# Linear attention and a gated feed-forward network on one core: the gates of the last four chunks as two pairs with seven block products instead of eight

## The chip, the cores and the metric

One NeuronCore of a Trainium2 chip runs the kernel. Its engines are TensorE (PE, matrix products into PSUM), VectorE (DVE), ScalarE (ACT), GpSimd (POOL) and SyncE (SP, which issues the DMAs); each has its own queue of instructions and works through it in order. The metric is the device time of one launch in microseconds, as a median of several runs.

## The reference

```
def phi(x): return np.where(x > 0, x, np.exp(x) - 1.0) + 1.0      # q, k, v: (8, 8, 576, 64) f32
q_p, k_p = phi(q), phi(k)
kv  = einsum('bhsd,bhse->bhde', k_p, v)
num = einsum('bhsd,bhde->bhse', q_p, kv)
den = einsum('bhsd,bhd->bhs', q_p, sum of k_p over s) + 1e-6
x   = (num / den), as 4608 tokens x 512
a, b = x @ w1, x @ w2                                             # w1, w2: 512 x 1024
out = (a * b) @ w3 @ w_out                                        # 4608 x 512, f32
```

## The kernel before, in words

The kernel multiplies w3 by w_out once (steps T3 and FW) and keeps the product as `wf_sb`. The 4608 tokens are 36 tiles of 128 tokens, in nine chunks of 512. For each of the eight batches b it loads q, k and v in halves h (steps LQ.b.h, LK.b.h, LV.b.h; each a transfer of 576 KB). EX (exponential, ACT), PT and PM (maximum and minimum, DVE) make phi of q and k in bf16, and VC casts v. KV and KB multiply k by v for one batch on PE. QD.b.h transposes phi(q) by a DMA. NT.t makes numerators and denominators of three tiles from t on (72 small matmuls on PE), and NM.t.0 to NM.t.2 divide (DVE). XD.c.m transposes half a chunk of x by a DMA, after the NM steps of its two tiles (in the first chunks XP does it on PE).

F.c.f makes 128 columns f of both gates for chunk c: four matmuls of 128x128 by 128x512 for a, four for b, an ACT copy of a to SBUF, and a DVE product of that copy and b's bank. O.t makes 128 rows of the result from `abs_` and `wf_sb` in eight matmuls of the same size and copies them out by ACT (.a) or DVE (.v), and S.t stores them. Q.35 is the last tile.

The order of everything is one list written out by hand, `ORDER`: each engine, and SP for its DMAs, gets its instructions in the order of that list. So a step that waits holds up everything behind it on its engine. Buffers are handed out in the order of the list too: 13 buffers "ld" for loads, each free again when both of its readers are done (EX and PT, or VC), four PSUM banks "mm" (one each for a and b of an F, for an O, and two for a KB), and two pairs of PSUM banks "at" (both pairs for one NT, free after NM.t.1 and NM.t.2). Result tiles take turns in five buffers `o_sb`.

`w_row` lays out the weights so that the two blocks of K that belong to one half of the contraction are next to each other.

Of the kernel before, what the change touches and what calls it, by code (L numbers as in the profile page):

```python
# [17 lines left out]
ORDER = """
L3.7 L3.4 L3.2 LO.1 I.0 H.1.1 H.3.0 H.1.2 I.1 T3.4.0.a H.2.3 T3.2.0.v T3.2.1.a T3.4.1.v H.1.4 C3.7.a
T3.7.0.v LO.0 CO.0.a LO.2 CO.1.v FW.2.0.a T3.7.1.a LO.3 FW.4.0.a CO.3.a LQ.0.0 L3.6 FW.7.0.a
PT.q.0.0 L3.1 FW.2.1.a FW.4.1.a EX.q.0.0 LQ.0.1 PM.q.0.0 CO.2.p FW.2.2.a FW.7.1.a FW.7.2.v FW.7.3.a
FW.4.2.a FW.4.3.v QP.0.0.v C3.6.a LK.0.0 T3.1.0.a T3.1.1.a PT.q.0.1 FW.2.3.v L3.3 L3.5 T3.6.0.v
T3.6.1.v EX.q.0.1 LK.0.1 FW.1.0.a FW.1.1.a PT.k.0.0 FW.1.2.a PM.q.0.1 FW.6.0.a FW.6.1.v FW.6.2.v
LH.0.0 EX.k.0.0 T3.3.0.a T3.3.1.a FW.1.3.a C3.5.v T3.5.0.a FW.6.3.v EX.k.0.1 PT.k.0.1 LV.0.0 LV.0.1
LH.0.1 FW.3.0.a FW.3.1.v T3.5.1.a FW.3.2.v FW.3.3.v PM.k.0.1 LA.0 LB.6 I.2 CA.0.p CB.6.p LB.7
PM.k.0.0 T3.0.0.a LA.1 FW.5.0.a VC.0.0.a QP.0.1.v FW.0.0.a FW.0.1.a KV.0.0.a LA.2 VC.0.1.v FW.5.1.v
T3.0.1.v KV.0.1.a NT.0 NM.0.0 NM.0.1 CB.7.p FW.0.2.a FW.0.3.a NM.0.2 FW.5.2.a FW.5.3.a LA.3 XP.0.a  # L30
CA.2.p XP.1.v ND.3 LB.2 CA.1.v XP.2.a LB.3 FS.0.0.0.0 FS.0.1.0.0 FS.0.1.1.0 FS.0.0.1.0 LQ.1.1 LK.1.0
XP.3.v FS.0.2.0.0 FS.0.2.1.0 FS.0.2.0.1 FS.0.2.1.1 CB.2.v FS.0.0.0.1 FS.0.0.1.1 FS.0.1.0.1
FS.0.1.1.1 FS.0.3.0.1 CB.3.v PT.q.1.1 CA.3.p F.0.4 EX.q.1.1 PM.q.1.1 PT.k.1.0 LQ.1.0 LV.1.0 PT.q.1.0
EX.k.1.0 FS.0.3.0.0 LK.1.1 F.0.5 F.0.6 PM.k.1.0 VC.1.0.v EX.q.1.0 PM.q.1.0 QP.1.1.a EX.k.1.1
FS.0.3.1.0 PT.k.1.1 LV.1.1 F.0.7 KV.1.0.a LQ.2.1 LQ.3.1 VC.1.1.a QP.1.0.a O.0.a PM.k.1.1 KV.1.1.v
LV.2.0 FS.0.3.1.1 EX.q.3.1 NT.4 NM.4.0 NM.4.1 O.1.a NM.4.2 EX.q.2.1 PT.q.2.1 LK.2.0 XP.4.a ND.7
XP.5.a LK.2.1 EX.k.2.1 LK.3.1 O.2.a PT.q.3.1 PT.k.2.1 LV.3.0 XP.6.v XP.7.v LV.2.1 EX.k.2.0 PM.k.2.1
# [19 lines left out]
S.19.s F.6.5 S.20.s NM.30.2 XD.7.1 F.6.6 F.6.7 O.24.a S.21.s O.25.v NT.33 NM.33.0 NM.33.1 NM.33.2
S.22.s S.23.s O.26.v O.27.v F.7.0 S.24.s XD.8.0 S.25.s F.7.1 F.7.2 F.7.3 F.7.4 F.7.5 F.7.6 XD.8.1
S.26.s S.27.s F.7.7 F.8.0 F.8.1 F.8.2 O.28.v O.29.v S.28.s O.30.a O.31.v F.8.3 S.29.s S.30.s S.31.s
F.8.4 F.8.5 F.8.6 F.8.7 O.32.v O.33.v S.32.s O.34.a S.33.s S.34.b Q.35  # L60
"""


# [1 line left out]
def kernel(  # L65
# [465 lines left out]

    def o_mm(t, cols):
        c0, m = divmod(t, CT)
        o_ps = mm_tile("o_ps")[:, 0:cols.stop - cols.start]
        for f in range(FC):
            nc.tensor.matmul(o_ps, abs_[c0][:, f, m * P:(m + 1) * P], wf_sb[:, f, cols],  # L536
                             start=(f == 0), stop=(f == FC - 1))
# [66 lines left out]
```

## Time and profile before

| | before |
|---|---|
| median of 3 runs | 240.89 us (240.65 to 241.69) |
| span of the profiled execution | 239.7 us |
| PE busy | 233.2 us (97%), 2276 matmuls |
| DVE busy | 151.0 us (63%) |
| ACT busy | 115.0 us (48%) |
| POOL busy | 8.1 us (3%) |
| main DMA queue (issued by SP) | 55.19 MB, packets in flight 78.5% of 16 engines' span |
| mean granted clock of PE | 0.999 |

The span runs from the first to the last instruction of the profiled execution; the median of the runs is 1.2 us above it. Busy time counts an engine's instructions alone. A PE that is busy is not yet at its best, since matmuls overlap; the distance from one matmul to the next tells what one costs. In the views a line number such as L483 is that of the kernel before: L483 the gate matmuls, L492 and L494 the copy and the product behind them, L536 and L543 the matmuls and the copy of O, L399 those of NT, L341 those of KB, L405 the divisions of NM, L286 and L294 PT and PM, L158 the loads, L386 and L463 the DMA transposes of QD and XD.

### The profile page before, as it was taken

To read this page: it belongs to the slowest core of one execution; us is meant where nothing else is said; L and a number is where in the kernel's file an instruction comes from. 1 tells how busy PE (TensorE), PEld (TensorE's weight loads), DVE (VectorE), ACT (ScalarE), POOL (GpSimd) and SP (SyncE) were. 2 spreads that over 40 slices of the span, in tenths; PEclk is the share of its full clock that TensorE was granted. 3 is DMA by queue.
4 is the path that set the end of the run, shared out by engine and by line. 5 is a ranking of instruction groups with operands and counts; after the bars stand their busy time and mean duration, and the time that the engine had idled before them with its cause. 6 is when DMAs were issued, how large, how long until landed. Compare 5 with 4: busy or idle time off the path is not lost.

```text
span 239.7 us, 5540 instructions
## 1 busy us (share of the span) xinstructions
PE 233.2 (97%) x2276; PEld 120.2 (50%) x2276; DVE 151.0 (63%) x278; ACT 115.0 (48%) x173; POOL 8.1 (3%) x15
## 2 busy tenths in 40 slices
PE   8899999999999999999999999999999999999994
...
DVE  0347787889999646877862588885546363433341
...
PEclk9999999999999999999999999999999999999999
DMA  6999999999996999999879959965293763005216
GB/s 241 402 406 397 379 375 390 390 390 389 396 332 137 158 357 247 323 406 296 190 106 192 392 123 262 320 116 131 52 178 69 174 157 88 3 0 125 50 24 154
DMA packets 52553, 55.81 MB, mean 233 GB/s; under 512 B 31280, under 2 KB 32560, under 8 KB 52528
## 3 DMA queue, kind: packets, MB, share of 16 engines
q1 hardware_dynamic: 52288, 55.19, 78.5%
...
## 4 chain that ended last, share of the span: by engine, by line
PE 96%; DVE 1%; ACT 1%; issue 0%
PE o_ps L536 26%; PE a_ps L483 25%; PE b_ps L483 24%; PE wf_ps L264 6%; PE nd L399 3%; PE w3p L252 3%; PE warm L149 2%; PE kbp L341 2%; PE a_ps L516 2%; PE b_ps L516 2%; PE xp L458 1%; PE qp L369 1%; PE kvp L341 1%; ACT wo_sb L218 0%; ACT w3b L238 0%; DVE w3t L253 0%
## 5 line engine op out<-in xcount | busy, mean ns | idle before, releaser
L483 PEld LDWEIGHTS <-w_sb 128*128 128x128 bf16 x544 | 52.6, 98 | 62.5 <-DVE xt L459 0.3
L494 DVE TENSOR_TENSOR ab<-a_sb,b_ps 128x512 bf16<-128x512 f32 x68 | 46.2, 686 | 39.9 <-PE b_ps L483 38.6
L492 ACT COPY a_sb<-a_ps 128x512 f32<-128x512 f32 x68 | 39.8, 586 | 64.0 <-PE a_ps L483 63.6
L483 PE MATMUL a_ps<-xt,w_sb 128*128 128x512 bf16 x272 | 69.9, 380 | 0.0
L483 PE MATMUL b_ps<-xt,w_sb 128*128 128x512 bf16 x272 | 69.8, 379 | 0.0
L536 PE MATMUL o_ps<-wf_sb,ab 128*128 128x512 bf16 (+2 forms) x304 | 65.2, 368 | 0.0
L536 PEld LDWEIGHTS <-ab 128*128 128x128 bf16 x304 | 28.4, 98 | 31.7 <-issue 0.4
L543 ACT COPY o_sb<-o_ps 128x512 f32<-128x512 f32 x22 | 12.9, 586 | 33.5 <-PE o_ps L536 26.7
L405 DVE TENSOR_TENSOR xn<-nd,r 128x512 bf16<-128x512 f32 (+2 forms) x47 | 23.8, 559 | 0.3
L274 ACT ACTIVATE ek<-k 128x1152 bf16<-128x1152 f32 x16 | 18.7, 1172 | 0.7 <-ACT ek L274 0.7
L274 ACT ACTIVATE eq<-q 128x1152 bf16<-128x1152 f32 x16 | 18.7, 1168 | 0.4 <-DMA q<-in_q_dram 0.4
L543 DVE COPY o_sb<-o_ps 128x512 f32<-128x512 f32 x13 | 9.0, 691 | 15.3 <-PE o_ps L536 12.6
L264 PE MATMUL wf_ps<-wo_sb,w3t 128*128 128x512 bf16 x64 | 15.6, 380 | 0.5 <-ACT wo_sb L218 0.5
L286 DVE TENSOR_SCALAR phq<-q 128x1152 bf16<-128x1152 f32 x16 | 12.0, 755 | 2.7 <-DMA q<-in_q_dram 2.7
L294 DVE TENSOR_TENSOR phk<-phk,ek 128x1152 bf16<-128x1152 bf16 x16 | 11.9, 750 | 1.8 <-ACT ek L274 1.7
L294 DVE TENSOR_TENSOR phq<-phq,eq 128x1152 bf16<-128x1152 bf16 x16 | 12.1, 755 | 1.0 <-ACT eq L274 0.8
L286 DVE TENSOR_SCALAR phk<-k 128x1152 bf16<-128x1152 f32 x16 | 12.0, 753 | 0.0
L264 PEld LDWEIGHTS <-w3t 128*128 128x128 bf16 x64 | 5.9, 98 | 5.8 <-issue 0.7
L328 ACT CAST vt<-v 128x1152 bf16<-128x1152 f32 x7 | 8.1, 1162 | 0.9 <-DMA v<-in_v_dram 0.9
L253 ACT CAST w3t<-w3p 128x512 bf16<-128x512 f32 x7 | 4.0, 587 | 9.3 <-PE w3p L252 7.4
L399 PEld LDWEIGHTS <-qt 64*64 64x64 bf16 x576 | 6.1, 106 | 4.3 <-issue 4.1
L399 PE MATMUL nd<-kv,qt 64*64 64x65 bf16 x576 | 7.6, 194 | 0.4 <-DVE w3t L253 0.4
...
## 6 DMA issues: line engine op xcount, KB each, us to landing
q<-in_q_dram SPq DMA_DIRECT2D x16, 576.0 KB, 8.3
k<-in_k_dram SPq DMA_DIRECT2D x16, 576.0 KB, 9.5
v<-in_v_dram SPq DMA_DIRECT2D x16, 576.0 KB, 10.5
out_dram<-o_sb SPq DMA_DIRECT2D x69, 128.0 KB, 2.5
...
```

The lines of the kernel that those rows point to most:

```text
L264: nc.tensor.matmul(wfs[i], w3ts[i][:, c, :], wo_sb[:, c, :], start=(c == 0), stop=(c == FC - 1))
L274: nc.scalar.activation(out=t, in_=raw[n, b, h], func=AF.Exp)
L286: (nc.gpsimd if e == "p" else nc.vector).tensor_scalar(out=by_set(n, t), in0=by_set("k", raw[n, b, h]), scalar1=0.0, scalar2=1.0, op0=ALU. ...
L294: nc.vector.tensor_tensor(out=t, in0=t, in1=by_set("k", es[n, b, h]), op=ALU.min)
L399: nc.tensor.matmul(dst[g * R:(g + 1) * R], qts[b, a // 2][rows, j, a % 2 * R:(a % 2 + 1) * R], kvs[b][rows, a // 2, a % 2, :], start=True, ...
L405: nc.vector.tensor_tensor(out=xn[:, :, a0:a1], in0=n4[:, :, :, 0:D], in1=r.unsqueeze(3).to_broadcast([P, 2, a1 - a0, D]), op=ALU.mult)
L483: nc.tensor.matmul(ops_[key][:, tiles.start * P:tiles.stop * P], w[:, w_row(kc), f * P:(f + 1) * P], xts[c0][:, tiles, kc, :], start=(kc = ...
L492: nc.scalar.copy(out=a_sbs[c0, f], in_=ops_[key])
L494: nc.vector.tensor_mul(out=abs_[c0][:, f, :], in0=a_sbs[c0, f], in1=ops_[key])
L516: nc.tensor.matmul(p, w[:, w_row(kc), f * P:(f + 1) * P], xts[c0][:, 2 * g:2 * g + 2, kc, :], start=(kc == 0), stop=(kc == KC - 1))
L536: nc.tensor.matmul(o_ps, abs_[c0][:, f, m * P:(m + 1) * P], wf_sb[:, f, cols], start=(f == 0), stop=(f == FC - 1))
L543: copy_of(e)(out=o_sbs[t], in_=o_ps)
```

## The change

The gates of chunks 5 and 6, and of chunks 7 and 8, are made in pairs. Each gate of a pair is a product of a 2x2 block matrix of weights (halves of K by halves of the 1024 columns) with a 2x2 block matrix of x (halves of K by the two chunks), by Strassen's scheme in Winograd's form: seven block products in place of eight.

- WS.side.i makes four sums of weight blocks for w1 (side 0) and w2 (side 1) on POOL (128x1024 bf16 each), eight instructions in all. They lie in four of the 13 "ld" buffers until the end of the last pair.
- WT.c.i makes four sums of x blocks of a pair on DVE (128x1024 bf16 each), eight in all, in two "ld" buffers for each pair.
- WP.c.f.side.i is one of the seven block products for a block of 128 columns f = 0 to 3: two matmuls of 128x128 by 128x512. So 2 pairs x 4 x 2 sides x 7 = 112 steps and 224 matmuls stand in place of 32 F steps with 256 matmuls. Products 1, 6, 7 and 4 add up in one PSUM bank of a pair "at", 5 and 3 in the other; product 2 takes a bank "mm". In between ACT copies the bank to SBUF after products 1, 5 and 6 (and 4 on side 0), and DVE adds a copy to a bank after products 2, 3 and 7. On side 1 each of these is followed by the DVE product of a and b, and after 4 by a product straight from the bank: 7 ACT copies and 10 DVE instructions for each f of a pair, where the four F steps that it replaces had 4 and 4.
- `o_mm` reads the gates of a pair from four more "ld" buffers.
- `ORDER` is another one from O.3 on. Loads, QD, NT and XD of all eight batches now stand ahead of the first WP but for XD.8.0 and XD.8.1; 14 O steps stand between the WP steps, and two more before the last of them.

```diff
@@ ORDER, cut to what stands between O.3 and the first products of a pair @@
...
-LV.3.1 O.3.a PT.k.2.0 LQ.2.0 S.0.s LQ.3.0 PM.k.2.0 PM.q.2.1 VC.2.0.v LV.4.1 F.1.0 F.1.1 PT.k.3.1
-PM.q.3.1 VC.3.0.a F.1.2 VC.2.1.a PT.q.2.0 F.1.3 LK.3.0 EX.q.2.0 PM.q.2.0 LQ.5.1 S.1.s S.2.s ND.8
-KB.2.a QD.2.0 EX.k.3.1 F.1.4 PT.q.3.0 EX.q.3.0 PT.k.3.0 PM.k.3.1 F.1.5 VC.3.1.v QD.2.1 EX.k.3.0
-PM.k.3.0 QD.3.1 F.1.6 F.1.7 O.4.a PM.q.3.0 PT.q.5.1 QD.3.0 NT.9 KB.3.a O.5.a NM.9.0 O.6.a NM.9.1
-NM.9.2 NT.12 NM.12.0 NM.12.1 NM.12.2 O.7.a XD.2.0 XD.2.1 LV.4.0 F.2.0 LQ.4.0 EX.q.5.1 F.2.1 NT.15
-S.3.s F.2.2 NM.15.0 F.2.3 LK.4.1 F.2.4 PM.q.5.1 F.2.5 VC.4.0.a LQ.4.1 LK.4.0 PT.k.4.0 EX.k.4.0
-PM.k.4.0 XD.3.0 PT.k.4.1 F.2.6 F.2.7 XD.3.1 LK.5.1 LK.5.0 F.3.0 PT.q.4.0 PT.q.4.1 F.3.1 EX.q.4.0
-F.3.2 PT.k.5.1 LK.7.0 O.8.a PT.k.5.0 EX.k.4.1 NM.15.1 NM.15.2 F.3.3 S.4.s EX.q.4.1 PM.k.4.1 EX.k.5.0
-LV.5.1 LV.6.0 S.5.s VC.4.1.v PM.q.4.0 EX.k.5.1 LQ.5.0 LV.5.0 S.6.s PM.k.5.1 F.3.4 PT.q.5.0 PM.q.4.1
-S.7.s S.8.s VC.5.0.v O.9.a EX.q.5.0 O.10.a O.11.a LQ.7.1 VC.5.1.v PM.q.5.0 QD.4.0 F.3.5 F.3.6
-PM.k.5.0 EX.k.7.0 KB.4.v PT.k.7.0 QD.4.1 S.9.s S.10.s S.11.s F.3.7 KB.5.a NT.18 XD.4.0 O.12.a
-PM.k.7.0 NM.18.0 NM.18.1 XD.4.1 QD.5.1 NM.18.2 O.13.a O.14.v O.15.a F.4.0 F.4.1 F.4.2 F.4.3 VC.6.0.a
-QD.5.0 LK.7.1 PT.k.7.1 F.4.4 EX.k.7.1 LK.6.0 PT.k.6.0 NT.21 NM.21.0 NM.21.1 NM.21.2 LQ.6.0 F.4.5
...
+LV.3.1 O.3.a PT.k.2.0 LQ.4.0 PM.q.2.1 PM.q.3.1 PT.k.3.1 F.1.2 LQ.2.0
+PT.q.2.0 LQ.3.0 PM.k.2.0 F.1.3 LK.3.0 S.3.s EX.q.2.0 PM.q.2.0 F.1.5 PT.k.3.0 PT.q.3.0 LK.4.0 EX.k.3.1
+F.1.0 VC.2.1.a VC.2.0.v EX.q.3.0 F.1.4 LQ.5.0 S.1.s QD.2.0 LV.4.1 QD.2.1 PM.q.3.0 LQ.4.1 F.1.1 EX.k.3.0
+S.0.s PM.k.3.0 EX.q.4.0 ND.8 PM.k.3.1 QD.3.1 KB.2.a VC.3.1.v F.1.6 F.1.7 WS.1.1.p QD.3.0 VC.3.0.a
+PT.k.4.0 EX.k.4.0 O.5.a NT.9 LV.5.0 NM.9.0 NM.9.1 NM.9.2 LV.6.1 KB.3.a XD.2.0 XD.2.1 PM.k.4.0 EX.q.5.0
+O.4.a NT.12 NM.12.0 S.2.s NM.12.1 LK.5.0 EX.q.4.1 NM.12.2 VC.5.0.v O.6.a PT.q.5.0 O.7.a PT.q.4.0
+WS.0.1.p LK.4.1 NT.15 LQ.5.1 PT.q.4.1 F.2.4 XD.3.0 NM.15.0 PM.q.4.0 NM.15.1 F.2.5 F.2.3 PM.q.5.0
+VC.4.1.v WS.0.2.p LV.5.1 XD.3.1 LQ.7.1 EX.k.4.1 QD.4.0 F.2.6 EX.k.5.0 PM.q.4.1 LK.6.0 LV.4.0 LK.5.1
+F.2.2 LK.7.0 WS.0.4.p PT.k.4.1 VC.5.1.v LQ.7.0 F.3.2 NM.15.2 PM.k.4.1 LQ.6.0 QD.4.1 EX.k.6.0 PT.k.5.0
+F.2.0 F.3.5 F.2.1 EX.q.5.1 EX.k.5.1 LK.6.1 XD.4.0 PT.q.5.1 PT.k.5.1 F.3.6 F.2.7 QD.5.0 VC.4.0.a PM.q.5.1
+PM.k.5.0 LV.6.0 F.3.1 KB.4.v EX.q.7.0 PM.k.5.1 LV.7.1 O.10.a KB.5.a PT.k.6.0 PT.q.7.0 NT.18 PT.k.7.0
+LV.7.0 PM.k.6.0 NM.18.0 QD.5.1 F.3.0 NM.18.1 S.5.s S.4.s NM.18.2 PT.q.7.1 VC.7.1.v VC.6.0.a S.7.s F.3.7
+LK.7.1 LQ.6.1 VC.7.0.a F.3.4 S.6.s EX.k.6.1 PT.q.6.0 NT.21 EX.q.6.0 O.8.a XD.4.1 NM.21.0 NM.21.1 XD.5.0
+EX.q.6.1 PM.q.6.0 PT.q.6.1 O.9.a PM.q.7.0 O.11.a VC.6.1.v PT.k.7.1 NM.21.2 PT.k.6.1 F.3.3 PM.k.6.1
+QD.7.0 S.11.s QD.6.0 F.4.7 S.10.s PM.q.6.1 NT.24 EX.k.7.1 EX.q.7.1 QD.6.1 KB.6.v EX.k.7.0 NM.24.0
+PM.q.7.1 QD.7.1 F.4.2 NM.24.1 F.4.3 S.8.s PM.k.7.0 NM.24.2 XD.6.0 PM.k.7.1 F.4.0 XD.5.1 F.4.1 NT.27
+WS.1.2.p NM.27.0 KB.7.a O.13.a NM.27.1 NM.27.2 NT.30 NM.30.0 NM.30.1 XD.6.1 XD.7.0 O.12.a NM.30.2
+WT.5.1.v F.4.5 XD.7.1 NT.33 WS.1.3.p NM.33.0 WT.5.2.v NM.33.1 NM.33.2 F.4.6 F.4.4 WP.5.0.1.1 WS.1.4.p
+WT.5.4.v WP.5.0.0.1 WT.5.3.v S.12.s WS.0.3.p O.14.v WP.5.0.0.6 WP.5.0.0.5 WP.5.0.1.5 WP.5.0.0.7 S.13.s
+WP.5.0.0.2 WP.5.0.1.6 WP.5.0.0.3 WP.5.0.0.4 WP.5.0.1.7 S.9.s WP.5.0.1.3 WP.5.1.0.1 O.19.a WP.5.0.1.4
+WP.5.1.0.6 WP.5.1.0.5 XD.8.1 WP.5.0.1.2 WP.5.1.1.1 WP.5.1.0.7 WP.5.1.1.5 XD.8.0 WP.5.1.1.6 WP.5.1.0.3
+WP.5.1.1.3 WP.5.1.0.4 WP.5.1.1.7 O.15.a WP.5.2.0.1 WP.5.1.1.4 O.18.a WT.7.1.v WP.5.2.1.1 WP.5.2.0.6
...
@@ the new steps @@
+    def s_WS(side, i, e):
+        w = (w1_sb, w2_sb)[side]
+        a, b, op = {1: (w_half(w, 0, 1), w_half(w, 1, 1), ALU.add),
+                    2: (ws_of(side, 1), w_half(w, 0, 0), ALU.subtract),
+                    3: (w_half(w, 0, 0), w_half(w, 0, 1), ALU.subtract),
+                    4: (w_half(w, 1, 0), ws_of(side, 2), ALU.subtract)}[i]
+        (nc.gpsimd if e == "p" else nc.vector).tensor_tensor(out=ws_of(side, i), in0=a, in1=b, op=op)
+
+    def s_WT(c0, i, e):
+        b11, b12, b21, b22 = x_half(c0, 0), x_half(c0 + 1, 0), x_half(c0, 1), x_half(c0 + 1, 1)
+        a, b = {1: (b12, b11), 2: (b22, xs_of(c0, 1)), 3: (b22, b12), 4: (b21, xs_of(c0, 2))}[i]
+        (nc.gpsimd if e == "p" else nc.vector).tensor_tensor(out=xs_of(c0, i), in0=a, in1=b, op=ALU.subtract)
+
+    def w_mm(ps, c0, f, side, i, first):
...
+        for r in range(2):
+            nc.tensor.matmul(ps, lhs[:, r, f * P:(f + 1) * P], rhs[:, :, r, :],
+                             start=(first and r == 0), stop=(r == 1), skip_group_check=not first)
+
+    def w_add(c0, f, side, ps, tmp, c, g):
+        nc.vector.tensor_tensor(out=tmp, in0=ps, in1=tmp, op=ALU.add)
+        if side == 0:
+            wtmp[c0, f, "a", c, g] = tmp
+        else:
+            nc.vector.tensor_mul(out=w_ab(c0, f)[:, c, g], in0=wtmp.pop((c0, f, "a", c, g)), in1=tmp)
+
+    def s_WP(c0, f, side, i, e):
+        q = c0, f, side
+        if i in (1, 5) and q not in wbank:
+            wbank[q] = at_tile("wp" + "ab"[side], ("wp",) + q)
+        if i == 2:
+            wbank[q + ("x",)] = mm_tile("wx" + "ab"[side], ("wx",) + q)
+        ps = wbank[q + ("x",)] if i == 2 else wbank[q][:, 0 if i in (1, 6, 7, 4) else 1]
+        w_mm(ps, c0, f, side, i, i in (1, 2, 5))
+        if i in (1, 5, 6):
+            t = wtmp[q + (i,)] = w_tmp({1: "e", 5: "phq", 6: "phk"}[i], "p" + str(i) + "ab"[side])
+            nc.scalar.copy(out=t, in_=ps)
+        elif i == 2:
+            w_add(c0, f, side, ps, wtmp.pop(q + (1,)), 0, 0)
+            give("mm", ("wx",) + q)
+        elif i == 3:
+            w_add(c0, f, side, ps, wtmp.pop(q + (6,)), 1, 0)
+        elif i == 7:
+            w_add(c0, f, side, ps, wtmp.pop(q + (5,)), 1, 1)
+        elif side == 0:
+            t = wtmp[c0, f, "a", 0, 1] = w_tmp("w3t", "p4a")
+            nc.scalar.copy(out=t, in_=ps)
+        else:
+            nc.vector.tensor_mul(out=w_ab(c0, f)[:, 0, 1], in0=wtmp.pop((c0, f, "a", 0, 1)), in1=ps)
+        if i == 4:
+            give("at", ("wp",) + q)
...
```

More of the change, by code (lines that the diff above doesn't have):

```diff
@@ L16 @@
 NCH = 512
+PAIRS = (5, 7)
 ORDER = """
 L3.7 L3.4 L3.2 LO.1 I.0 H.1.1 H.3.0 H.1.2 I.1 T3.4.0.a H.2.3 T3.2.0.v T3.2.1.a T3.4.1.v H.1.4 C3.7.a
[L23 to L26, printed above, removed]
@@ L57 @@
[L57 to L60, printed above, removed]
+T3.7.0.v LO.0 CO.0.a LO.2 CO.1.v FW.2.0.a T3.7.1.a LO.3 FW.4.0.a CO.3.a LQ.0.0 L3.6 FW.7.0.a PT.q.0.0
+L3.1 FW.2.1.a FW.4.1.a EX.q.0.0 LQ.0.1 PM.q.0.0 CO.2.p FW.2.2.a FW.7.1.a FW.7.2.v FW.7.3.a FW.4.2.a
@@ new lines @@
+CB.7.p FW.0.2.a FW.0.3.a NM.0.2 FW.5.2.a FW.5.3.a LA.3 XP.0.a CA.2.p XP.1.v ND.3 LB.2 CA.1.v XP.2.a LB.3
+FS.0.0.0.0 FS.0.1.0.0 FS.0.1.1.0 FS.0.0.1.0 LQ.1.1 LK.1.0 XP.3.v FS.0.2.0.0 FS.0.2.1.0 FS.0.2.0.1
+FS.0.2.1.1 CB.2.v FS.0.0.0.1 FS.0.0.1.1 FS.0.1.0.1 FS.0.1.1.1 FS.0.3.0.1 CB.3.v PT.q.1.1 CA.3.p F.0.4
+EX.q.1.1 PM.q.1.1 PT.k.1.0 LQ.1.0 LV.1.0 PT.q.1.0 EX.k.1.0 FS.0.3.0.0 LK.1.1 F.0.5 F.0.6 PM.k.1.0
+VC.1.0.v EX.q.1.0 PM.q.1.0 QP.1.1.a EX.k.1.1 FS.0.3.1.0 PT.k.1.1 LV.1.1 F.0.7 KV.1.0.a LQ.2.1 LQ.3.1
@@ new lines @@
+WP.5.2.0.4 WP.5.2.1.4 O.16.a WP.5.2.1.3 WP.5.3.0.1 WT.7.2.v WP.5.2.0.2 WP.5.3.0.5 WP.5.3.1.1 S.18.s
+WP.5.3.0.6 WT.7.4.v WP.5.2.1.2 WP.5.3.1.5 WP.5.3.1.6 WP.5.3.0.3 WP.5.3.0.7 S.14.s O.17.v WP.5.3.0.4
+WP.5.3.1.7 S.19.s WP.5.3.0.2 WP.7.0.0.1 WP.5.3.1.3 WP.5.3.1.4 WT.7.3.v WP.7.0.0.2 WP.7.0.0.5 WP.7.0.0.6
+O.27.v WP.7.0.1.1 S.16.s WP.7.0.0.7 WP.5.3.1.2 WP.7.0.1.6 WP.7.0.1.5 WP.7.0.0.4 S.17.s WP.7.0.1.7
+WP.7.0.0.3 O.25.v WP.7.0.1.3 WP.7.1.0.1 WP.7.0.1.4 S.25.s O.23.a WP.7.1.1.5 WP.7.1.0.5 WP.7.1.1.1
@@ L61 @@
+WP.7.3.1.3 S.22.s S.28.s O.31.v S.31.s O.30.a O.33.v O.32.v S.29.s S.33.s S.30.s S.32.s O.34.a S.34.b
+Q.35
 """
@@ L530, in s_FP, with ab_of @@
             f_out(c0, f, side)
+    def ab_of(c0, f):
+        if c0 in PAIRS:
+            return quads[c0, f % 4][:, 0, f // 4]
+        if c0 - 1 in PAIRS:
+            return quads[c0 - 1, f % 4][:, 1, f // 4]
+        return abs_[c0][:, f]
     def o_mm(t, cols):
@@ L535, in o_mm @@
         for f in range(FC):
-            nc.tensor.matmul(o_ps, abs_[c0][:, f, m * P:(m + 1) * P], wf_sb[:, f, cols],
+            nc.tensor.matmul(o_ps, ab_of(c0, f)[:, m * P:(m + 1) * P], wf_sb[:, f, cols],
                              start=(f == 0), stop=(f == FC - 1))
@@ L544, in s_O @@
         give("mm", "o_ps")
+        c0 = t // CT - (t // CT - 1 in PAIRS)
+        if c0 in PAIRS:
+            n = uses["o", c0] = uses.get(("o", c0), 0) + 1
+            if n == 2 * CT:
+                for f in range(FC // 2):
+                    give("ld", ("abq", c0, f))
     def store(queues, t, o_sb, cols):
@@ L563, in s_Q, with late, w_half, x_half @@
             store((nc.sync, nc.scalar), t, o_sb, slice(pieces[0][0], pieces[-1][1]))
+    quads, wsum, xsum, wbank, wtmp, uses = {}, {}, {}, {}, {}, {}
+    def late(key, n):
+        t = take("ld", key, [P, HW], F32, key[0]).bitcast(BF16)[:, 0:n * NCH]
+        return t
+    def w_half(w, k, fh):
+        return w[:, 2 * k:2 * k + 2, fh * NCH:(fh + 1) * NCH]
+    def x_half(c0, k):
+        return xts[c0][:, :, k::2, :]
+    def ws_of(side, i):
+        key = ("ws", side, (i - 1) // 2)
+        if key not in wsum:
+            wsum[key] = late(key, 4).rearrange("p (i r n) -> p i r n", i=2, r=2)
+        return wsum[key][:, (i - 1) % 2]
@@ new lines, in xs_of @@
+    def xs_of(c0, i):
+        key = ("xs", c0, (i - 1) // 2)
+        if key not in xsum:
+            xsum[key] = late(key, 4).rearrange("p (i m r n) -> p i m r n", i=2, m=CT, r=2)
+        return xsum[key][:, (i - 1) % 2]
+    def s_WS(side, i, e):
[5 more added lines that the diff above has]
+        (nc.gpsimd if e == "p" else nc.vector).tensor_tensor(out=ws_of(side, i), in0=a, in1=b, op=op)
@@ new lines, in s_WT @@
+    def s_WT(c0, i, e):
[3 more added lines that the diff above has]
+    def w_mm(ps, c0, f, side, i, first):
+        w = (w1_sb, w2_sb)[side]
+        lhs = {1: lambda: w_half(w, 0, 0), 2: lambda: w_half(w, 1, 0), 3: lambda: ws_of(side, 4),
+               4: lambda: w_half(w, 1, 1), 5: lambda: ws_of(side, 1), 6: lambda: ws_of(side, 2),
+               7: lambda: ws_of(side, 3)}[i]()
+        rhs = {1: lambda: x_half(c0, 0), 2: lambda: x_half(c0, 1), 3: lambda: x_half(c0 + 1, 1),
+               4: lambda: xs_of(c0, 4), 5: lambda: xs_of(c0, 1), 6: lambda: xs_of(c0, 2),
+               7: lambda: xs_of(c0, 3)}[i]()
+        for r in range(2):
+            nc.tensor.matmul(ps, lhs[:, r, f * P:(f + 1) * P], rhs[:, :, r, :],
+                             start=(first and r == 0), stop=(r == 1), skip_group_check=not first)
@@ new lines, in w_tmp, with w_ab @@
+    def w_tmp(kind, name):
+        t = take(kind, None, [P, FC, P] if kind == "w3t" else [P, HW], BF16, name)
+        if kind == "w3t":
+            t = t.rearrange("p c t -> p (c t)")
+        return t.bitcast(F32)[:, 0:NCH]
+    def w_ab(c0, f):
+        if (c0, f) not in quads:
+            quads[c0, f] = late(("abq", c0, f), 4).rearrange("p (c g n) -> p c g n", c=2, g=2)
+        return quads[c0, f]
+    def w_add(c0, f, side, ps, tmp, c, g):
[4 more added lines that the diff above has]
+            nc.vector.tensor_mul(out=w_ab(c0, f)[:, c, g], in0=wtmp.pop((c0, f, "a", c, g)), in1=tmp)
```

39 lines of the change are left out of this document (22 added, 17 removed).

## The prediction

> **What bounds the kernel now.** First the busy shares and the slices, then who PE waited for, then the chain.
>
> ```profile
> PE 233.2 (97%) x2276; PEld 120.2 (50%) x2276; DVE 151.0 (63%) x278; ACT 115.0 (48%) x173; POOL 8.1 (3%) x15
> PE   8899999999999999999999999999999999999994
> DVE  0347787889999646877862588885546363433341
> PEclk9999999999999999999999999999999999999999
> DMA  6999999999996999999879959965293763005216
> PE warm L149 <- DVE zero L136: 1.2, 1, 1.2
> ...
> PE w3p L252 <- DVE w3t L253: 0.3, 1, 0.3
> PE 96%; DVE 1%; ACT 1%; issue 0%
> ```
>
> PE is the bound. Its waits are five rows from 1.2 to 0.3 us, all in the first part, and the chain that ended last is PE for 96% of the span. The clock is granted in full. But the DMA row is at nine tenths or more for almost the whole first half, and DVE runs high up to slice 20: there is little behind PE to spare there, and plenty after slice 28. I call 0.5%, 1.2 us, what a measurement of this kernel can tell from no change.
>
> **What PE saves.** The distance between matmuls of 512 columns comes from the chain in order of time:
>
> ```profile
> 59.93 0.86 PE a_ps L483 x4
> 213.66 6.91 PE o_ps L536 x32
> 136.43 0.58 PE L399 MATMUL nd<-kv,qt 64*64 64x65 bf16 x48
> 66.92 0.78 PE L341 MATMUL kbp<-vt,phk 64*64 64x65 bf16 x72
> ```
>
> 6.91 / 32 = 0.216 us for one. 256 matmuls become 224, so PE's work falls by 32 x 0.216 = 6.9 us. Sums in PSUM add no matmul, and no other PE step changes.
>
> To see what the new order asks of the others I set up PE's own timetable by counting: an F or an O is 8 x 0.216 = 1.73 us, a KB 0.75, an NT 0.55 (rows above, less their overlap). F.1 starts at 59.93. Before NT.21 the old order has 29 F, 12 O, 4 KB and 4 NT steps: 59.93 + 50.1 + 20.7 + 3.0 + 2.2 = 135.9; the third row above has it at 136.43, so the count is good to 0.5 us. In the new order NT.21 stands behind only 23 F, 5 O, 4 KB and 4 NT: 59.93 + 39.7 + 8.6 + 3.0 + 2.2 = 113.5, with the same 0.5 us 113.9. NT.33, the last of the attention, moves from 190 to 138.
>
> **What the transfers need by then.** A pair wants two chunks of x before its first product, so all eight batches must be loaded and transposed some 50 us sooner. SP's queue and the 16 DMA engines behind it are common to loads, transposes and stores.
>
> ```profile
> 50.00:70.00 20.00, 20.00 (x286) 10.22 (x284) 18.29 (x37) 17.06 (x24) 0.00 (x0) 1.00 1.05 391
> 59.90:120.20 60.30, 60.30 (x709) 28.74 (x709) 47.63 (x85) 36.75 (x54) 0.00 (x0) 1.00 1.00 284
> q<-in_q_dram SPq DMA_DIRECT2D x16, 576.0 KB, 8.3
> out_dram<-o_sb SPq DMA_DIRECT2D x69, 128.0 KB, 2.5
> L158 SPq DMA_DIRECT2D v<-in_v_dram x1: 1267/1267/1267, 50.7 to 50.7; - x1
> DMA to landing us min/median/max: 12.1/12.1/12.1
> L386 SPq DMA_TRANSPOSE qt<-phq x12: 1242/1362/2040, 68.5 to 175.8; - x12
> DMA to landing us min/median/max: 3.2/3.6/5.0
> L463 SPq DMA_TRANSPOSE xt<-xn x14: 1232/1251/3275, 78.3 to 195.2; - x14
> ```
>
> The first two are stretches (length; busy time of PE, weight loads, DVE, ACT and POOL; clock, share of the DMA engines, GB/s). With loads alone the queue moves 391 GB/s at a share of 1.05: it is full, and 576 KB (590,000 bytes) take 1.51 us. A store of one tile (two of 128 KB) takes 0.67. A transpose I put at SP's own time for it, 1.30 for QD and 1.25 for XD. LV.3.1, the last load that both orders share, is issued at 50.7 and lands at 62.8; everything behind it on SP lands after that.
>
> In the new order QD.5.1, which NT.21 needs, stands behind 25 loads, 7 QD, 5 XD and 4 stores: 25 x 1.51 + 8 x 1.30 + 5 x 1.25 + 4 x 0.67 = 57.1 us, so it is through at 119.9, where PE wants it at 113.9: 6.0 us late, even if SP never leaves the queue empty. The same sum makes XD.2.1 (10 loads, 4 QD, 2 XD, 3 stores) 3.4 us late for F.2.4 at 84.2, and QD.7.1 0.4 us late for NT.30 at 134.3; the peak is at NT.21. In the old order QD.5.1 had 18 loads, 7 QD, 6 XD and 12 stores, 51.8 us: due at 114.6 for an NT.21 at 136.4, with 22 us to spare. That is where the cover went. To the 6.0 I add 1.4 us, by which a QD's slowest landing (5.0) exceeds its median (3.6): these stand between loads. So 7.4 us late. PE has no idle time to give back, and what it loses at NT.21 it keeps.
>
> The ends: if the transposes took nothing from the loads, 25 x 1.51 + 4 x 0.67 = 40.4, and PE waits for nothing. At the 284 GB/s which the mixed stretch 59.9 to 120.2 moved, the 19.5 MB (14.7 loads, 3.7 transposes at two bytes, 1.0 stores) take 68.6 us and NT.21 is 17.5 us late. I stay near the lower middle, since that stretch also held SP's waits for data.
>
> **DVE and ACT up to the pairs.** Moved with the loads are their EX, PT, PM and VC steps.
>
> ```profile
> L494 DVE TENSOR_TENSOR ab<-a_sb,b_ps 128x512 bf16<-128x512 f32 x68 | 46.2, 686 | 39.9 <-PE b_ps L483 38.6 <-ACT a_sb L492 0.8 <-issue 0.3
> L492 ACT COPY a_sb<-a_ps 128x512 f32<-128x512 f32 x68 | 39.8, 586 | 64.0 <-PE a_ps L483 63.6
> L294 DVE TENSOR_TENSOR phq<-phq,eq 128x1152 bf16<-128x1152 bf16 x16 | 12.1, 755 | 1.0 <-ACT eq L274 0.8
> 59.59 0.75 DVE L294 TENSOR_TENSOR phk<-phk,ek 128x1152 bf16<-128x1152 bf16 x1
> 60.26 0.76 DVE L286 TENSOR_SCALAR phk<-k 128x1152 bf16<-128x1152 f32 x1
> 77.58 1.95 DVE L405 TENSOR_TENSOR xn<-nd,r 128x512 bf16<-128x512 f32 x4
> ```
>
> Queued back to back a PT or PM costs 0.67 (60.26 - 59.59), a gate product about 0.60, an NT with its NM steps 0.73 + 1.95 = 2.7. From O.3 to NT.33 the new order gives DVE 21 PT, 23 PM and 7 VC (34.2), 30 products (18.0), 8 trios (21.4) and some 3 us of small ones: 76.6 us in the 78 that PE's timetable leaves. It fits without reserve. While PE waits for the transfers DVE waits for the same loads or catches up, so I cost it at nothing beyond the lateness above; if the loads came in time, DVE would cost 1 to 2 us by itself. ACT has 64.0 us idle on L492 alone, and its 24 more copies (7 x 8 for 32) are 24 x 0.59 = 14 us there. The stores S.5, S.4 and S.7 stand behind QD.5.1 on SP, so O.8, whose buffer S.5 must empty, is late by about as much as NT.21, not on top of it.
>
> **The pairs themselves.** For each f of a pair PE has 28 x 0.216 = 6.05 us, DVE 10 x 0.60 to 0.686 = 6.0 to 6.9, ACT 7 x 0.59 = 4.1. DVE alone would set the pace, but 14 O steps (24 us of PE) stand between: PE 48.4 + 24.2 = 72.6 us, DVE 48 to 55, plus 8 copies of O and 4 WT, 56 to 63, or 87% at most. So the bound is the chain inside one bank: product 1, copy, product 6, copy, product 7, add, product 4. Between product 6 and product 7 stand an ACT copy (0.59) and the drain of the last matmul; ORDER puts about three products (1.3 us) there, and at some places two. With nothing lost it is 0, with 0.2 us lost in each of 16 half-units 3.2; I take 1.0, since the spacing covers one copy, not two queued. No row of before shows a DVE product with both f32 inputs in SBUF (24 of these); L494 at 686 ns is the nearest. [...]
>
> The eight WT are bf16 of 1024, 0.67 each as PM; they lie where DVE has room. Four WS buffers held to the end leave 9 of 13 for loads; in flight at 12.1 us and 1.51 each are eight, so that costs nothing as long as ACT and DVE keep up.
>
> **The sum.** 239.7 - 6.9 (products) + 7.4 (transfers) + 1.0 (chain in the banks) = 241.2 for the span, and the runs' median stands 1.2 above the span: 242.4. So the saving is spent, and a little more.
>
> [...] The eight WS run on POOL, three of them early, as soon as a buffer is free.
>
> ```profile
> 11.51 0.68 DVE L218 CAST wo_sb<-wo 128x1024 bf16<-128x1024 f32 x1
> 11.72 1.37 POOL L218 CAST wo_sb<-wo 128x1024 bf16<-128x1024 f32 x1 [10.07 <-DMA wo<-in_moe_w_out_dram]
> 30.44 1.04 POOL L222 CAST w_sb<-wa 128x1024 bf16<-128x1024 f32 x1 [16.99 <-DMA wa<-in_moe_w_dram]
> ```
>
> Beside a DVE cast POOL's took 1.37 in place of 1.04, and DVE's took 0.68 as elsewhere: here POOL paid. No row shows a DVE instruction that starts during one of POOL's. If DVE then waited, eight sums of at least 1.04 us could hold it 8.3 us, three of them (3.1 us) before NT.12. [...]
>
> **The rivals.**
> - The transfers come nearly in time and most of the saving stays. For it: transposes and loads may overlap, and PE has never waited for a transfer in the old order. Against it: the stretch with loads alone is full at 391 GB/s, and QD.5.1 has seven loads more in front of it and 22 us less. If the lateness is 3 us and the chain costs 0.5: 240.9 - 6.9 + 3.5 = 237.5. It decides from a lateness under 5. 0.28.
> - POOL holds DVE as above: 245.5. It decides where PM meets a sum while DVE has under 1 us of reserve. 0.12.
> - The chain in the banks costs 0.2 us at all 16 half-units and O steps meet it too: 3.2 in place of 1.0, 244.6. 0.05.
>
> **How the numbers follow.** The forecast's own case, transfers 5 to 10 us late, is 240.0 to 245.0 and has 0.55; of this 0.24 lies within 1.2 us of 240.9 (up to 242.1) and 0.31 above. Faster is the first rival, 0.28. Slower is 0.31 + 0.12 + 0.05 = 0.48. The range goes from 237.5, the first rival's own point, to 246.5, the POOL rival's point and 1 us: outside are half of the first rival's lower part and the far end of the mixed-rate bound, some 0.2 together.
>
> **What would show it.** The PE waits should grow from 2.8 us to about 11, led by NT (L399) and by gate matmuls in chunk 2, 3 and 4 whose releaser is a DMA transpose, or a DVE or ACT step that itself waited for a load; NT.21 should start near 121 us. DMA share should stay at 1.0 from 10 to 130 us and PE's busy digits dip below nine between 75 and 130. After the first product of a pair, waits of PE should be short ones on ACT copies and DVE adds, about 1 us in all. The prediction is wrong on the low side if NT.21 starts before 118, and on the high side if DVE's PM rows grow well above 755 ns beside POOL.

## The result, and the profile after

| | before | after |
|---|---|---|
| median of 4 runs | 240.93 us (240.65 to 241.69) | 278.82 us (277.15 to 281.61) |
| ratio after / before | | 1.1532, 95% interval 1.1463 to 1.1601 |
| span of the profiled execution | 239.7 us | 275.3 us |

The forecast was 242.4 us with a range up to 246.5. The changed kernel is 15% slower; one of its four runs (281.61 us) was in a slower state, 1.6% above the fastest, and the ratio leaves it out. Its page of the profile: busy shares, slices, and the chain that ended last.

```profile
PE 236.5 (86%) x2244; PEld 117.5 (43%) x2244; DVE 195.9 (71%) x334; ACT 128.2 (47%) x197; POOL 26.9 (10%) x23
PE   8899999996889969998799977775877887869993
DVE  0376879896999996889999954736766737555741
POOL 1200430002510060028000000000000000000000
PEclk9999999998899988999999999999999999999999
DMA  7999999999999999999999930032110030104346
PE 64%; DVE 14%; DMA 9%; ACT 8%; issue 3%; DVEq 0%; ACTq 0%
```

PE has its 32 matmuls less, but about a quarter of slices 24 to 36 is empty, in a stretch where neither DVE, nor POOL, nor the DMA engines are full. The front (slices 10 to 20) has smaller gaps, and there the DMA row is full throughout. Two windows and the first product of a pair, in the columns of the prediction's windows:

```profile
10.00:157.00 147.00, 135.89 (x1797) 71.46 (x1798) 126.42 (x229) 88.31 (x129) 25.91 (x16) 0.98 1.08 312
157.00:275.00 118.00, 92.28 (x417) 39.71 (x414) 67.84 (x104) 36.34 (x64) 0.00 (x0) 1.00 0.24 56
156.87 0.59 PE L638 MATMUL wpb<-xt,w_sb 128*128 128x512 bf16 x2
```

The same count of steps that put NT.21 at 113.5 to 113.9 us puts the first product at 141.9 to 142.4 us if PE waits for nothing (32 F, 10 O, 6 KB and 9 NT behind 59.93). I take 142.1, so the two losses that follow are good to 0.3 us. It came at 156.87: 14.8 us lost ahead of the pairs. With the whole saving the span would be 239.7 - 6.9 = 232.8, so PE needs 90.7 us from there to the end. It took 275.3 - 156.87 = 118.4: 27.7 us lost behind the first product. 232.8 + 14.8 + 27.7 = 275.3.

Of the 14.8 us, PE's waits between 60 us and the first product are 9.74 by their rows: 4.47 for transfers (`xt` and `qt`) and 5.27 for VectorE. About 3 us more are two stretches in which PE ran at half its rate; the last section has them.

The waits of PE name the second loss (engine, line and tile, releaser: us in total, times, longest):

```profile
PE wpb L638 <- DVE p6b L654: 5.0, 5, 2.1
PE wpa L638 <- DVE p6a L654: 4.7, 4, 2.6
PE a_ps L495 <- DMA xt<-xn: 3.5, 2, 2.5
PE b_ps L495 <- DVE ab L506: 3.2, 2, 2.4
PE wpb L638 <- ACT p5b L670: 3.1, 7, 0.7
PE wpa L638 <- ACT p6a L670: 2.4, 4, 0.8
```

A releaser "p6" under a product seems to fit the chain that the prediction priced (product 6, copy, product 7). It doesn't, as the timeline shows (start, length, engine; in brackets the idle time before and what ended it):

```profile
160.09 0.59 ACT L670 COPY p6a<-wpa 128x512 f32<-128x512 f32 x1 [1.51 <-PE wpa L638]
160.73 0.59 PE L638 MATMUL wpa<-xs,ws 128*128 128x512 bf16 x2 [0.67 <-ACT p6a L670]
161.36 0.59 ACT L670 COPY p5a<-wpa 128x512 f32<-128x512 f32 x1 [0.68 <-PE wpa L638]
161.99 0.59 PE L638 MATMUL wpa<-xs,ws 128*128 128x512 bf16 x2 [0.24 <-ACT p5a L670]
...
190.42 0.68 DVE L654 TENSOR_TENSOR p6a<-wpa,p6a 128x512 f32<-128x512 f32 x1
191.16 0.59 PE L638 MATMUL wpa<-xs,w_sb 128*128 128x512 bf16 x2 [2.64 <-DVE p6a L654]
```

The order has WP.5.0.0.6, WP.5.0.0.5, then WP.5.0.1.5 and WP.5.0.0.7. So the product at 160.73 is product 5, which opens the second bank and needs nothing of product 6; it still starts 0.64 us after the copy p6a began to read the first bank. The product at 161.99 is 7, in the first bank; it waits for the copy of product 5, from the second. At 191.16 a product 4 (first bank) waits 2.64 us for the sum "p6a", which DVE makes from the second bank after product 3. The two banks are one tile `[P, 2, 512]`, and each product waits for the newest reader of the tile, whichever bank was read. Set beside the order, 37 products started over 60 ns later than the usual 0.216 us behind the matmul before them, 27.7 us in all. For 33 of them, 27.2 us, the trace names a releaser, and each time it is a reader of the other bank; none is the product's own chain. The other four, 0.5 us, have no releaser. (The waits of the profile count from the modelled end of a matmul; for the same 33 they sum to 21.9 us.)

### The profile page after: what moved, and what is told of

Read it like the earlier page. It is cut to its first block, busy times and chain, and to the rows that moved or that the text cites. A ratio compares the mean times of both kernels' runs of the same rounds, so it can differ in the third digit from the quotient of the medians.

```text
span 275.3 us, 5566 instructions
## 1 busy us (share of the span) xinstructions
PE 236.5 (86%) x2244; PEld 117.5 (43%) x2244; DVE 195.9 (71%) x334; ACT 128.2 (47%) x197; POOL 26.9 (10%) x23
## 4 chain that ended last, share of the span: by engine, by line
PE 64%; DVE 14%; DMA 9%; ACT 8%; issue 3%; DVEq 0%; ACTq 0%
PE o_ps L555 18%; PE a_ps L495 8%; PE b_ps L495 8%; PE wpb L638 7%; PE wpa L638 6%; PE wf_ps L276 5%; DMA q<-in_q_dram 4%; DMA xt<-xn 2%; PE w3p L264 2%; DMA qt<-phq 2%; PE warm L161 2%; PE nd L411 1%; ACT p5b L670 1%; DVE ab L506 1%; DVE xn L417 1%
## 5 line engine op out<-in xcount | busy, mean ns | idle before, releaser
L495 PEld LDWEIGHTS <-w_sb 128*128 128x128 bf16 x288 | 28.4, 101 | 42.3 <-issue 11.1
L495 PE MATMUL a_ps<-xt,w_sb 128*128 128x512 bf16 x144 | 38.6, 393 | 3.5 <-DMA xt<-xn 3.5
L495 PE MATMUL b_ps<-xt,w_sb 128*128 128x512 bf16 x144 | 38.7, 393 | 3.2 <-DVE ab L506 3.2
L555 PE MATMUL o_ps<-wf_sb,ab 128*128 128x512 bf16 x160 | 37.7, 379 | 0.3 <-DVE ab L506 0.3
L504 ACT COPY a_sb<-a_ps 128x512 f32<-128x512 f32 x36 | 20.9, 584 | 19.7 <-PE a_ps L495 19.6
L555 PE MATMUL o_ps<-wf_sb,abq 128*128 128x512 bf16 (+2 forms) x144 | 29.3, 355 | 0.0
L506 DVE TENSOR_TENSOR ab<-a_sb,b_ps 128x512 bf16<-128x512 f32 x36 | 24.1, 681 | 5.0 <-PE b_ps L495 3.8
L555 PEld LDWEIGHTS <-abq 128*128 128x128 bf16 x144 | 13.5, 98 | 14.5
L638 PE MATMUL wpa<-xs,ws 128*128 128x512 bf16 x48 | 14.2, 378 | 5.5 <-ACT p6a L670 2.2
L638 PE MATMUL wpb<-xs,ws 128*128 128x512 bf16 x48 | 14.2, 378 | 5.0 <-ACT p5b L670 2.8
L638 PEld LDWEIGHTS <-w_sb 128*128 128x128 bf16 x96 | 9.3, 97 | 21.1 <-issue 10.7
```

What stands on the lines that cost most here:

```text
L495: nc.tensor.matmul(ops_[key][:, tiles.start * P:tiles.stop * P], w[:, w_row(kc), f * P:(f + 1) * P], xts[c0][:, tiles, kc, :], start=(kc = ...
L504: nc.scalar.copy(out=a_sbs[c0, f], in_=ops_[key])
L506: nc.vector.tensor_mul(out=abs_[c0][:, f, :], in0=a_sbs[c0, f], in1=ops_[key])
L555: nc.tensor.matmul(o_ps, ab_of(c0, f)[:, m * P:(m + 1) * P], wf_sb[:, f, cols], start=(f == 0), stop=(f == FC - 1))
L638: nc.tensor.matmul(ps, lhs[:, r, f * P:(f + 1) * P], rhs[:, :, r, :], start=(first and r == 0), stop=(r == 1), skip_group_check=not first)
```

## The experiments

**Theory A**: the tile of two banks makes products wait for each other. **Rivals B and C**: their own copies and sums are late; or adding up in a bank costs PE. For the front: **theory T**, the transfers as a whole are too slow for a start at 142; its rival, GpSimd's sums hold VectorE, which was a rival of the prediction too.

### One-bank tiles

The pool of the two pairs "at" is closed at the first product of a pair, and four single banks take its place; each is given back by itself, after product 3 or 4. (No wait of the trace above is for a bank of an earlier unit, so that cannot be what helps.)

```diff
-        if i in (1, 5) and q not in wbank:
-            wbank[q] = at_tile("wp" + "ab"[side], ("wp",) + q)
+        if "one" not in pools:
+            two.close()
...
+        bank = 0 if i in (1, 6, 7, 4) else 1
+        if i in (1, 5):
+            wbank[q + (bank,)] = take("one", ("wp", bank) + q, [P, NCH], F32, "wp" + "ab"[side] + str(bank))
-        ps = wbank[q + ("x",)] if i == 2 else wbank[q][:, 0 if i in (1, 6, 7, 4) else 1]
+        ps = wbank[q + ("x",)] if i == 2 else wbank[q + (bank,)]
```

> The changed kernel with one difference: each half unit of a pair takes two separate PSUM tiles of one bank (products 1, 6, 7, 4 in the one, 5, 3 in the other) in place of one tile of two banks. Products, copies, sums and their order stay. Theory A (the two-bank tile makes every product wait for the newest reader of the other bank, too): of the 27.7 us lost after the first product only the waits on a product's own chain stay, 1 to 5 us, so the median falls from 278.8 to 252 to 257 us, and the first product still starts near 156.9 us. Rival B (the copies and sums of a product's own bank are late, since the order spaces them too closely, or VectorE is full): the waits are on each product's own chain and stay with separate tiles; 270 us or more. Rival C (the accumulation in a bank with start left out costs TensorE itself): the products stay long and the time stays above 270 us.

252.83 us (251.38 to 254.34), 1.048 of before (1.0439 to 1.0521). The two longest waits of PE, the only row with a product of a pair, the first product, and the stretch of the pairs:

```profile
PE b_ps L497 <- DVE ab L508: 3.6, 3, 2.4
PE a_ps L497 <- DMA xt<-xn: 2.5, 1, 2.5
...
PE wpb L640 <- DVE xn L419: 0.3, 1, 0.3
159.81 0.39 PE L640 MATMUL wpb<-xt,w_sb 128*128 128x512 bf16 x1 [0.28 <-DVE xn L419]
160.00:250.00 90.00, 86.22 (x408) 39.85 (x414) 65.80 (x104) 35.17 (x64) 0.00 (x0) 1.00 0.31 72
```

The row with a product of a pair, 0.3 us, is the wait of the very first. From the first product to the end PE took 250.8 - 159.81 = 91.0 us, against 90.7 with nothing lost. Theory A is shown, B and C are out: the same products, copies, sums and order run without a wait, and the saving of 6.9 us is there in full behind the first product. What tied the two halves together was the shared tile: with it 33 products waited 27.2 us for readers of the other half, and with a tile for each half none did. Rotating products through several banks was not enough by itself: both kernels do that, at 1.1532 and at 1.048 of before.

What is left, 11.4 us over the 241.43 of before measured beside it, lies in the front: its first product came at 159.8. That is 2.9 us later than in the changed kernel, with the same order and code up to there; two executions of one front differ by that much.

### The sums of weights on VectorE, and left out

```diff
-WS.1.1.p ... WS.0.1.p ... WS.0.2.p ... WS.0.4.p ... WS.1.2.p ... WS.1.3.p ... WS.1.4.p ... WS.0.3.p
+WS.1.1.v ... WS.0.1.v ... WS.0.2.v ... WS.0.4.v ... WS.1.2.v ... WS.1.3.v ... WS.1.4.v ... WS.0.3.v
```

Without the sums these eight steps are gone from the order, and `w_mm` takes plain blocks:

```diff
-        lhs = {..., 3: lambda: ws_of(side, 4), ..., 5: lambda: ws_of(side, 1), 6: lambda: ws_of(side, 2), ...
+        lhs = {..., 3: lambda: w_half(w, 0, 1), ..., 5: lambda: w_half(w, 0, 0), 6: lambda: w_half(w, 0, 1), ...
```

> The kernel with one-bank tiles, with the eight sums of weights on VectorE in place of GpSimd, at the same places in the order. If GpSimd's sums stretch VectorE's work beside them (by my count 9.9 us of VectorE in the changed kernel's trace) and this delays the front: the rows beside them go back from up to 2.7 us to about 0.75 us, VectorE takes on eight sums of about 0.6 us, the first product starts 3 to 8 us earlier than with one-bank tiles alone, and the time falls by as much (to 245 to 252 us). If the transfers of q and k alone set the front: the first product starts within 1 us of that of the kernel with one-bank tiles, and the time is the same within 1 us.

> The kernel with one-bank tiles, without the eight sums of weights on any engine (the products take plain blocks of the weights in their place, so this part of the computation is left out). Its first product's start, beside 156.9 us, is the front without GpSimd's sums: 4 to 9 us earlier if their price on VectorE sets the front, within 1 us of the others if the transfers alone do. What then remains against 142.1 us (TensorE's work without waits) is the transfers' part: 6 to 11 us.

Here the rows of the changed kernel, first. GpSimd's sums, VectorE's instructions beside them, and the means of their groups:

```profile
74.07 2.52 POOL L622 TENSOR_TENSOR ws<-ws,w_sb 128x1024 bf16<-128x1024 bf16 x1
74.53 0.68 DVE L506 TENSOR_TENSOR ab<-a_sb,b_ps 128x512 bf16<-128x512 f32 x1
75.13 2.08 DVE L306 TENSOR_TENSOR phq<-phq,eq 128x1152 bf16<-128x1152 bf16 x1
L306 DVE TENSOR_TENSOR phq<-phq,eq 128x1152 bf16<-128x1152 bf16 x16 | 15.6, 979 | 0.4 <-ACT eq L286 0.4
L622 POOL TENSOR_TENSOR ws<-w_sb 128x1024 bf16<-128x1024 bf16 x4 | 9.0, 2253 | 51.5 <-DMA out_dram<-o_sb 28.7 <-ACT vt L340 20.1 <-ACT a_sb L504 2.8
```

A sum took 2.1 to 2.65 us, and PM took 2.08 beside it in place of 0.755: it ended 0.6 us after the sum did. Eight instructions of VectorE were stretched so, by 9.9 us in all. The gate product at 74.53, inside the same sum, kept its 0.68. All eight that were stretched (three PM, three PT, two VC) work on tiles in SBUF alone; the gate products that start inside a sum (74.53, 100.27 and two from 127.66) have b's PSUM bank as one input, and kept 0.68 (1.27 for the two). What decides it was not shown: no run changed the place of an input.

Yet it cost little. With the sums on VectorE (PM back at 751 ns) the time was 250.47 us (250.17 to 252.73), 1.0402 of before (1.0361 to 1.0443), and the first product came at 157.32, 2.5 us earlier; without any sums it was 252.4 us in one run. That kernel's first product:

```profile
159.63 0.60 PE L633 MATMUL wpb<-xt,w_sb 128*128 128x512 bf16 x2
```

This is 0.2 us before the kernel that has them on GpSimd. The changed kernel, with GpSimd's sums, had come at 156.87, before either. So the 3 to 8 us that the stretching was to cost are not there; 2.5 us is less than the scatter of one front, and I draw nothing from it. Something else held all of them to 157 to 160. Against 142.1 that leaves 17.5 us without any sums, where 6 to 11 were expected.

### Half of the late loads

```diff
+        if half(key):
+            dst, src = dst[:, 0], src[:, 0]
         nc.sync.dma_start(out=dst, in_=src)
```

`half` holds for q, k and v of batches 4 to 7; EX, PT and VC read the loaded half twice.

> The kernel with one-bank tiles and GpSimd's sums; of the 24 loads of q, k and v of batches 4 to 7 only the first half of each is loaded, and its reader takes that half twice (so the second half of these inputs is left out; every instruction on the engines keeps its size). Theory T (the transfers as a whole set when the first product starts: 147 us at a mean DMA share of 1.08 from 10 to 157 us): 7.1 MB less, 18 us at the 391 GB/s of the full slices, so the first product starts near TensorE's own 142 us, at 142 to 148 in place of 159.8 us, and the time falls to 235 to 242 us. Rival (VectorE, stretched by GpSimd's sums, sets it as well): the first product stays at 152 us or later here, and moves only where the sums leave GpSimd.

> The same halved loads, with the sums of weights on VectorE. Theory T alone: the first product within 1 us of the kernel with halved loads and GpSimd's sums. [...]

One run each, 246.3 us with the sums on GpSimd, 239.29 with them on VectorE. Of each kernel, in that order, the first product, the stretch ahead of it, and the longest row of PE's waits:

```profile
153.42 0.39 PE L651 MATMUL wpb<-xt,w_sb 128*128 128x512 bf16 x1
10.00:146.00 136.00, 125.59 (x1718) 67.34 (x1718) 120.38 (x213) 86.75 (x126) 25.75 (x16) 1.00 0.96 276
PE b_ps L508 <- DVE ab L519: 4.8, 5, 1.4
```

```profile
146.32 0.60 PE L644 MATMUL wpb<-xt,w_sb 128*128 128x512 bf16 x2 [1.27 <-DVE xn L423]
10.00:146.00 136.00, 131.57 (x1796) 70.33 (x1794) 118.81 (x233) 88.14 (x129) 6.92 (x8) 1.00 1.03 287
PE b_ps L501 <- DVE ab L512: 1.8, 2, 1.4
```

No transfer of q, k, v or x is left among PE's waits of the front in either, and with 18 us less to load the start moved 6.4 and 11.0 us ahead: the transfers held it back. But theory T is not the whole: my numbers for the first of the two (142 to 148, and 235 to 242 us) were a miss, and the rival's condition came true there: 153.4 with GpSimd's sums, 146.3 without, 7.1 us apart, in waits for VectorE. The four kernels together say how the two causes add up: with full loads GpSimd's sums cost 2.5 us or nothing, with half loads 7. They lie side by side; the longer one sets the start, and taking away the shorter one alone brings nothing. (Each start is of one execution; 6.4 and 7.1 us are clear of the 2.9 by which one front scattered.)

### Fewer transposing transfers

```diff
-XD.2.0 XD.2.1 ... XD.3.0 ... XD.3.1 ... XD.4.0 ... XD.4.1
+XP.8.a XP.9.a XP.10.a XP.11.a ... XP.12.a XP.13.a ... XP.14.a XP.15.a ... XP.16.a XP.17.a ... XP.18.a XP.19.a
```

> One-bank tiles, sums on VectorE, and the six transposing transfers of x of chunks 2 to 4 replaced by twelve transposes on TensorE with copies on ScalarE. Theory T: two such transfers alone took 2.6 us of all 16 DMA engines, so six free about 7.8 us and the first product starts 5 to 8 us earlier than the 157.3 us of the kernel with the transfers, less up to 3 us for 48 small transposes on TensorE where it does not wait anyway: 243 to 248 us. If VectorE or the order of the loads sets the front: the same start within 1 us, or later by the 3 us.

243.30 us (242.95 to 243.63), 1.008 of before (1.0051 to 1.0109), with all of the data loaded. The first product and the transposes on PE:

```profile
150.19 0.61 PE L634 MATMUL wpb<-xt,w_sb 128*128 128x512 bf16 x2 [0.27 <-DVE xn L413]
80.48 1.00 PE L466 MATMUL xp<-ident,xn 128*128 128x128 bf16 x8 [0.43 <-DVE xn L413]
```

It starts 7.1 us earlier than with the transfers (157.32), although PE has 48 small matmuls more; eight take 1.00 here and 0.61 in four later rows, so they are about 4 us of PE, 146 in its timetable. That is 1.2 us for each of the six transfers, and the front is now about 4 us from what PE itself needs. Up to 1.5 us of the 7.1 are a stretch of half rate at 83.4 us that the kernel with the transfers had and this one lacks. This fits theory T, in a version of the change that loses only 0.8%. It does not separate two ways in which a transposing transfer can delay the loads: by its share of the DMA engines, or by its wait for data in SP's queue, where the loads stand behind it (from 50 to 160 us SP waited 18.2 us ahead of such transfers of x with the six, 10.5 without).

### One pair at the end

The front must be early only because two pairs need all of x by 142. So: the kernel before, with chunks 7 and 8 alone as a pair (16 matmuls, 3.5 us), one-bank tiles, the sums on VectorE.

```diff
+PAIRS = (7,)
-O.22.v ... F.6.0 ... NT.33 ... F.7.0 ... F.8.7
+WS.0.1.v F.6.0 WS.1.1.v ... F.6.7 NT.33 ... XD.8.1 O.22.a O.23.a WT.7.1.v ... WP.7.0.0.1 ...
```

> The kernel before, with only its last two chunks as a pair by seven products, in one-bank tiles, the weight sums on VectorE beside chunk 6, and the order up to chunk 5 that of the kernel before. It saves 16 matmuls of 0.216 us, 3.5 us. If the loss of the changed kernel lies in the shared two-bank tile and in the front's new order alone: 237 to 239 us, faster than before by 2 to 4 us. If the seven-product form itself cannot run without waits (chains of a copy and a sum per bank on ScalarE and VectorE): 242 us or more.

246.35 us (245.50 to 248.61), 1.0226 of before (1.0187 to 1.0266): slower than before, in the range of the second case. PE lost 7.8 us behind the first product, most of it at:

```profile
PE wpa L630 <- DVE xs L619: 2.2, 1, 2.2
PE wpb L630 <- DVE p5b L646: 1.6, 1, 1.6
PE wpa L630 <- ACT p1a L667: 1.4, 1, 1.4
```

These are real waits of a chain: the first sum of x blocks needs the last transfer of chunk 8, and copies and sums come late at more places, where fewer O steps stand between the products than in the big change. VectorE was not full: it was busy for 30.3 of the 41.9 us from the first product to the last. I ordered the end anew, by the durations and distances of these traces. The new order also gives all four copies of O between the products to ACT, where five of six were on VectorE.

```diff
-QD.7.0 NT.30 NM.30.0 NM.30.1 ... F.6.5 ... F.6.6 ... F.6.7 NT.33 ... XD.8.1 ... O.22.a O.23.a ... WP.7.0.0.1
+QD.7.0 WS.0.3.v NT.30 NM.30.0 NM.30.1 NM.30.2 F.6.6 F.6.5 NT.33 ... XD.8.1 ... F.6.7 WT.7.1.v O.22.a O.23.a ... WP.7.0.1.1
```

> The kernel with one pair at the end, its last part ordered anew: the last attention steps and the transposing transfers of chunk 8 stand right behind the transfers of q that they need, before the last two units of chunk 6, and the seven products are spaced by the measured rows (a product 0.43, a copy 0.49 on ScalarE, a sum 0.61 on VectorE, some 0.65 to 0.73 us from one engine to the next). If the 7.8 us that TensorE lost after the first product in the first try are a matter of order: at most 1 us is lost there, 236.5 to 239.5 us, faster than before by 1.5 to 4 us. If the seven-product form itself needs more of VectorE than it has: 242 us or more.

239.17 us (238.45 to 239.78) against 241.24 (240.48 to 242.24): 0.9913, 95% interval 0.9887 to 0.9938. It beats both kernels. Its busy shares, its slices of PE, and the one wait that a product of a pair still has:

```profile
PE 230.3 (97%) x2260; PEld 118.7 (50%) x2260; DVE 168.6 (71%) x308; ACT 124.4 (52%) x191; POOL 7.9 (3%) x15
PE   8899999999999999999999999999999999999994
PE wpa L630 <- DVE xs L619: 0.4, 1, 0.4
```

0.5 us is lost behind the first product, with VectorE busy for 27.3 of the 31.8 us of the pair. So the form can run nearly without waits, and the 7.8 us were a matter of order and of which engine copies; the two are not separated. Of the 3.5 us 2.1 arrived; 0.5 of the rest is the wait above, and where the other 0.9 went I did not follow further.

## Why the prediction was wrong, step by step

- **What PE saves**: right. 6.9 us were put down, and with one-bank tiles the end takes 91.0 us where 90.7 were counted.
- **The pairs themselves**: the step that failed. "The bound is the chain inside one bank" left out what the tile was. The chain was costed at 1.0 us with 3.2 as its end, and PE lost 27.7, of which 27.2 in waits that the trace puts down to readers of the other bank. "The spacing covers one copy" was true for the chain (nothing is lost on it with one-bank tiles); the spacing between neighbouring products of the two banks of one unit, none at all in 18 of 59 places, was never priced. The code said it: `wbank[q][:, 0 ...]` and `[:, 1]` slice one tile. The third rival (0.2 us at each half unit) had the place right and the mechanism and the size wrong: 27.7 / 16 is 1.7 us. The DVE product with both f32 inputs in SBUF, which no row of before showed, was costed rightly at 686 ns, those of L494: it took 692 ns.
- **What the transfers need by then**: right in kind, too small. QD.5.1 was said to be through at 119.9 and to land by 121.3. Its row, its landing (the line ends in min, median and max), and NT.21, which PE began at 124.43:

```profile
L398 SPq DMA_TRANSPOSE qt<-phq x1: 2888/2888/2888, 117.9 to 117.9; - x1
DMA to landing us min/median/max: 7.9/7.9/7.9
125.85 0.38 PE L411 MATMUL nd<-kv,qt 64*64 64x65 bf16 x23 [1.01 <-DMA qt<-phq]
```

  It was issued at 117.9, before 119.9, and landed 7.9 us later, at 125.8, where 5.0 was the slowest of before. The sum charged a transpose with SP's 1.3 us; among loads it cost more. And I stopped at one step: "the peak is at NT.21" was wrong, since 10 to 12 us of lateness there grew to 14.8 at the first product. The whole front shows it: 1.08 x 147 = 159 us of the DMA engines passed before the first product, and 132 us between 10 and 142 hold that only at a share of 1.20, where the stretch with loads alone had shown 1.05. NT.21's 10 to 12 us lie between the 7.4 that I took and the 17.5 by 284 GB/s; the stretch from 59.9 to 120.2 moved 308 after the change. The transfers are not all of the 14.8 us: 4.47 are waits of PE for them by name, 5.27 for VectorE, and about 3 the half rate, which the sum did not have.
- **DVE and ACT up to the pairs** at nothing: this could pass only where the transfers were later still. VectorE was stretched by 9.9 us, and this shows as 7.1 us once the loads are halved. Without GpSimd's sums the first product still came 4.2 us after 142.1 there, with every wait of PE there on VectorE (which then makes the sums itself), where 1 to 2 us had been allowed.
- **POOL**: a sum took 2.1 to 2.65 us, not 1.04, and PM beside one took 2.08 in place of 0.755. The rival's 245.5 is 242.4 and 3.1, three sums at the 1.04 of POOL's casts. As the rival that sets the time it failed: the delay of VectorE was there, and longer than 8.3 us, at 9.9, but the transfers covered it.
- **What would show it**: NT.21 near 121 (124.4) and digits under nine between 75 and 130 came about. So did PM above 755 ns, named as a sign of a higher time; the time was higher, but for another reason. "Short waits, about 1 us in all" behind the first product was the sign that failed, by 27 us.
